# Attention, gated experts and a channel mix on one core: keys split on 128 partitions at once, their halves placed by transfers, and the first batch's steps in a given order

## The chip, the core and the metric

The kernel runs on one core of a Trainium2 chip. The metric is the device time of one execution in microseconds (us). TensorE is called PE, VectorE DVE, ScalarE ACT, GpSimd POOL, and SP is the queue from which nearly all DMA transfers are issued. A change of about 0.5% is what a measurement of this kernel can tell from none.

## What is computed

```python
def sm_attn(qq, kk, vv):
    s = scale * np.matmul(qq, kk.transpose(0, 1, 3, 2))
    a = softmax(s)
    return np.matmul(a, vv)
p_packed = sm_attn(p, k, v)                 # 8 batches, 8 heads, 576 tokens, 32 packed rows
x = sm_attn(q, p_packed, p_packed)          # then heads side by side: 576 x 512 for each batch

for e in range(4):                          # four experts, causal attention of width 64
    q, k, v = x @ wq[e], x @ wk[e], x @ wv[e]
    a = softmax(causal(scale * (q @ k.T)))
    out += gate[e] * (a @ v @ wo[e])        # gate: the two largest of x @ w_gate

xk, xr = mixes of out and out one token earlier (mu_k, mu_r)
k = np.maximum(xk @ w_k, 0.0)
result = sigmoid(xr @ w_r) * ((k * k) @ w_v)
```

All of it is float32. A number is carried as a high part `h` (type fp32r) and a low part `l` = x - h where the kernel writes "split", and a product is then three matmuls: h times h, h times l, l times h.

## The kernel before, in words

The program has two halves. In the first, up to about 400 us, the eight batches pass through these steps, each a Python generator that records its instructions:

- `front(b, g)`, for the two head groups g of a batch: loads, the scores of the packed rows (`eight`, L220), their softmax (L268 to L276, ACT L273), the transposes of the weights (L280) and their copy `aT`, the product with v (L289), `pp` (L296), its transpose (L301) and copy `ppT`; then the second scores `s2` (L220 on `qT`), transposed in blocks by DVE into `st` (L308), block maxima `m` (L311), subtraction (L313), Exp on ACT (L316), `ppT` times the expert weights `wa` (L220 on `wa`, split on ACT L319 and DVE L320 into `PWh` and `PWl`), the block sums (L323 to L328), the scaling (L329), the transposition back into `a2` (L332) and its split into `A2h` (L205) and `A2l` (L335). In batch 0 the subtraction, scaling and split run on DVE and ACT; in the others on POOL.
- `values(b)` (L357): expert values and gate logits, then the gates on DVE.
- `project(b, ep)` (L412), for the two pairs of experts: queries (x = 0), then keys (x = 1), 24 matmuls of 128x288 each into one PSUM tile. The 128 partitions of that tile are two experts of 64. For the keys each expert was copied to `ks` (ACT L430, 64 partitions) and its rest taken to `kl` (DVE L431, 64 partitions), and one transfer for each expert put the high part on the other 64 partitions of `ks` (L433, L434). For the queries, copy and rest go over 128 partitions (L424, L425), and two transfers place the halves.
- `soft(b, e, group)`: causal scores (L472), the masked maximum on DVE (L490), Exp on ACT (L494), and one small transfer, the corner (L501, `ms<-ms`).
- `turn(b, e, group)`: transposes of the weights (L515, and L522 for a block that holds the corner) and their copies `tb`; `pair_out(b, ep)`: the product with the values (L557), its factor (L568, `cx`, `cb`), and differences of tokens to DRAM (L592).
- `fold()`: 24 pieces of w_k and w_r are loaded (`raw`, L775), turned from 64-bit into 32-bit numbers (`decode`, L625 to L655, on DVE, POOL and ACT), split, multiplied by the expert output weights `wo` (L709) and stored.

The second half, from about 400 us on, multiplies with the folded weights (L868, L888, L929) and is not touched but for a buffer.

What sets the order: every step of every generator has a time in a unit of one twentieth of a batch (`FRONT_T`, `G1_T`, `VAL_T`, `PROJ_T`, `SOFT_T`, `TURN_LAG`, `OUT_LAG`, `FOLD_0`, `FOLD_T`) and is recorded in the order of these times, with priorities (`PR`, `PR0`) for the builder's scheduler, which then sets the order of each engine. At run time each engine takes its instructions in that order and waits on semaphores. Before the first loads have landed, PE multiplies zeros (`WARM` times, L168).

## Time and profile before

| | |
|---|---|
| median of 3 runs | 794.79 us (791.86 to 794.84) |
| the profiled execution | 789.45 us |
| its span, first to last instruction | 787.7 us |
| PE busy | 751.6 us (95%) |
| DVE, ACT, POOL busy | 477.4, 448.7, 384.5 us |
| mean granted clock of PE | 0.987 |
| moved by DMA | 148.35 MB |

The profile is of one execution. Its busy times say how long an engine had an instruction in work; a wait names the instruction whose semaphore came last. Two levels of TensorE's clock occur: 1.00 is 2.4 GHz and 0.50 is 1.2 GHz.

### The profile page before, as it was taken

To read this page: it belongs to the slowest core of one execution; us is meant where nothing else is said; L and a number is where in the kernel's file an instruction comes from. 1 tells how busy PE (TensorE), PEld (TensorE's weight loads), DVE (VectorE), ACT (ScalarE), POOL (GpSimd) and SP (SyncE) were. 2 spreads that over 40 slices of the span, in tenths; PEclk is the share of its full clock that TensorE was granted. 3 is DMA by queue.
4 is the path that set the end of the run, shared out by engine and by line. 5 is a ranking of instruction groups with operands and counts; after the bars stand their busy time and mean duration, and the time that the engine had idled before them with its cause. 6 is when DMAs were issued, how large, how long until landed. Compare 5 with 4: busy or idle time off the path is not lost.

```text
span 787.7 us, 15356 instructions
## 1 busy us (share of the span) xinstructions
PE 751.6 (95%) x5504; PEld 617.7 (78%) x5504; DVE 477.4 (61%) x1174; ACT 448.7 (57%) x1029; POOL 384.5 (49%) x484
## 2 busy tenths in 40 slices
PE   6789989999999999998999999999999999999998
PEld 4476968869697887877678888888888888888886
DVE  4979896979868668677767978787581111111111
ACT  2357677678767768786633532422967755555400
POOL 7358776764777635253601533631267443344610
PEclk9599999999999999999999999999999999999999
DMA  9856473655637353315459785867889565555511
GB/s 320 302 151 194 139 226 104 190 151 177 207 105 222 97 166 91 83 43 170 150 201 309 299 296 185 279 196 244 309 286 344 159 187 154 171 177 171 156 67 54
DMA packets 92396, 148.35 MB, mean 188 GB/s; under 512 B 9376, under 2 KB 64160, under 8 KB 90016
## 3 DMA queue, kind: packets, MB, share of 16 engines
q1 hardware_dynamic: 92176, 147.36, 58.7%
q8 instruction: 44, 0.72, 0.4%
q14 instruction: 32, 0.26, 0.1%
q10 hardware_dynamic: 144, 0.00, 0.0%
HBM read 87.04 MB, written 50.33 MB: 174 GB/s over the span
## 4 chain that ended last, share of the span: by engine, by line
PE 74%; DVE 11%; DMA 5%; POOL 4%; ACT 3%; issue 2%; SPq 0%; POOLq 0%; DVEq 0%; ACTq 0%
PE one L929 25%; PE big L888 8%; PE one L888 8%; PE one L557 5%; PE big L412 4%; PE one L868 4%; PE big L868 4%; DMA ms<-ms 4%; PE one L709 3%; PE one L357 3%; PE one L515 2%; PE one L472 2%; DVE ms L490 2%; ACT ms L494 1%; PE big L220 1%
## 5 line engine op out<-in xcount | busy, mean ns | idle before, releaser
L934 DVE TENSOR_TENSOR ring<-one,ring 128x512 f32<-128x512 f32 x36 | 24.9, 692 | 168.3 <-PE one L929 158.8
L929 PE MATMUL one<-wvh,yh 128*128 128x512 f32 x288 | 112.0, 389 | 0.0
L929 PE MATMUL one<-wvl,yh 128*128 128x512 f32 x288 | 112.0, 389 | 0.0
L929 PE MATMUL one<-wvh,yl 128*128 128x512 f32 x288 | 112.0, 389 | 0.0
L494 ACT ACTIVATE ms<-ms,nb 128x192 f32<-128x192 f32 (+3 forms) x128 | 78.4, 616 | 21.3 <-DVE nb L490 21.2
L211 POOL TENSOR_TENSOR yl<-yvh,yh 128x1024 fp32r<-128x1024 f32 (+1 forms) x24 | 49.1, 2060 | 44.7 <-ACT yh L914 24.6
L205 ACT COPY tb<-one 64x128 f32<-64x128 f32 (+5 forms) x208 | 61.4, 362 | 11.3 <-PE one L522 11.2
L640 POOL TENSOR_TENSOR dcx<-dcx,dcu 128x256 f32<-128x256 f32 x40 | 30.7, 768 | 66.1 <-DVE dcu L634 53.5
L929 PEld LDWEIGHTS one<-wvh,yh 128*128 128x128 f32 x288 | 54.1, 188 | 11.3
L929 PEld LDWEIGHTS one<-wvl,yh 128*128 128x128 f32 x288 | 54.1, 188 | 11.3
L929 PEld LDWEIGHTS one<-wvh,yl 128*128 128x128 f32 x288 | 54.1, 188 | 11.1
L211 POOL TENSOR_TENSOR yl<-yvl,yh 128x1024 fp32r<-128x1024 f32 x16 | 38.2, 2396 | 41.0 <-ACT yh L914 19.7
L515 PE MATMUL one<-ident,ms 128*128 128x128 f32 x320 | 53.1, 281 | 3.1 <-ACT ms L494 3.0
L557 PE MATMUL one<-tb,vg 128*64 128x320 f32 (+4 forms) x448 | 53.6, 362 | 0.6 <-DVE nb L490 0.4
L490 DVE CUSTOM_DVE_ANT_0 ms<-one,mstrip 128x192 f32<-128x192 f32 (+2 forms) x96 | 43.5, 481 | 15.9 <-PE one L472 15.2
L557 PEld LDWEIGHTS one<-tb,vg 128*64 128x64 f32 x448 | 33.3, 136 | 18.3 <-issue 1.7
L515 PEld LDWEIGHTS one<-ident,ms 128*128 128x128 f32 x320 | 36.2, 141 | 13.5 <-ACT ms L494 8.3
L211 POOL TENSOR_TENSOR dt<-cb 128x192 f32<-128x192 f32 (+1 forms) x48 | 31.4, 684 | 30.9 <-DVE cb L575 24.2
L1051 ACT ACTIVATE ring<-ring 128x1024 f32<-128x1024 f32 x18 | 19.0, 1059 | 34.9 <-DMA ring<-rscr 34.9
L472 PE MATMUL one<-ks,qs 128*128 128x192 f32 (+3 forms) x128 | 36.6, 300 | 0.4 <-ACT vg L205 0.3
L522 PE MATMUL one<-ident,ms 128*128 128x128 f32 x96 | 27.4, 287 | 9.3 <-DMA ms<-ms 8.7
L661 POOL TENSOR_TENSOR wl<-wc,wh 128x256 fp32r<-128x256 f32 x48 | 34.9, 751 | 0.3
(208 smaller groups left out, 2071.1 us busy)
## 6 DMA issues: line engine op xcount, KB each, us to landing
yscr<-y SPq DMA_DIRECT2D x48, 384.0 KB, 3.5
dl<-dscr SPq DMA_DIRECT2D x40, 256.0 KB, 5.8
yvh<-yscr SPq DMA_DIRECT2D x10, 1024.0 KB, 5.9
kT<-in_k_dram SPq DMA_DIRECT2D x16, 576.0 KB, 4.2
qT<-in_q_dram SPq DMA_DIRECT2D x16, 576.0 KB, 5.7
rscr<-rr SPq DMA_DIRECT2D x12, 768.0 KB, 4.4
ring<-rscr SPq DMA_DIRECT2D x36, 256.0 KB, 2.9
out_dram<-ring SPq DMA_DIRECT2D x36, 256.0 KB, 3.2
```

The lines of the kernel that those rows point to most:

```text
L205: return nc.scalar.copy(o, x)
L211: nc.gpsimd.tensor_tensor(o, x, y, op=op)
L412: nc.tensor.matmul(ps[:, 512 * hf : 512 * hf + SH], ww[:, g, :], xx[:, g, :], start=i == 0, stop=i == 3 * NG - 1,)
L472: nc.tensor.matmul(ps[:, po : po + kn], qs[:, qo : qo + P], keys[:, ko : ko + kn], start=x == 0, stop=x == 1,)
L490: nc.vector.tensor_tensor_reduce(halves(mv) if last else mv, sv, halves(mk) if last else mk, op0=ALU.add, op1=ALU.min, scale=-SC, scalar=3 ...
L494: nc.scalar.activation(to, mv, AF.Exp, bias=nb[:n], scale=-1.0, accum_out=bat["sums"][:n, i, e : e + 1],)
L515: nc.tensor.transpose(ps[:, at + j * P : at + (j + 1) * P], ms[:, j * P : (j + 1) * P], ident)
L557: nc.tensor.matmul(av[64 * ee : 64 * ee + 64, qo - lo : hi - lo], vg[:, j, HD * (2 * ep + ee) : HD * (2 * ep + ee + 1)], tslice(tabs[ee], ...
L661: nc.gpsimd.tensor_sub(l, x, f32(h))
L868: nc.tensor.matmul(po, dx[:, NS * t + s, t0 : t0 + P], wpart("r", s, wx, t), start=n == 0, stop=n == 3 * KT - 1,)
L888: nc.tensor.matmul(po.rearrange("p (b n) -> p b n", b=2), wpart("k0" if f < 4 else "k1", s, wx, t)[:, f % 4 * P : f % 4 * P + P], dx[:, :, ...
L929: nc.tensor.matmul(ps, a[:, f, P * t : P * t + P], wres["v"][b][:, f, :], start=n == 0, stop=n == 3 * NFT - 1,)
```

## The change

The keys: one copy and one subtraction over 128 partitions into `kx` and `lk`, and six transfers for each pair of experts (two for each expert's high part, one for its rest), in place of two copies, two subtractions and two transfers.

```diff
                 if x == 0:
                     z = qt.rearrange("p (e s) -> p e s", e=2)
                     l = ex.tile([P, S], F32R, tag="l", name=nm("l"), bufs=1)
+                    h = z[:, 0, :]
                 else:
-                    z = ks = ex.tile([P, 2, S], F32R, tag="ks", name=nm("ks"))
+                    ks = ex.tile([P, 2, S], F32R, tag="ks", name=nm("ks"))
+                    l, h = (ex.tile([P, S], F32R, tag=n_, name=nm(n_), bufs=1) for n_ in ("lk", "kx"))
+                nc.scalar.copy(halves(h), pv)
+                nc.vector.tensor_sub(halves(l), pv, halves(f32(h)))
                 if x == 0:
-                    nc.scalar.copy(halves(z[:, 0, :]), pv)
-                    nc.vector.tensor_sub(halves(l), pv, halves(f32(z[:, 0, :])))
                     evac(E_Z, z[64:, 1, :], f32(z[64:, 0, :]))
+                    moves = [(z[64:, 0, :], l[:64]), (z[:64, 1, :], l[64:])]
                 else:
+                    moves = []
                     for e in range(2):
                         r = slice(64 * e, 64 * e + 64)
-                        nc.scalar.copy(halves(z[r, e, :]), pv[r])
-                        nc.vector.tensor_sub(halves(kl[r, e, :]), pv[r], halves(f32(z[r, e, :])))
-                top, bot = (l, l) if x == 0 else (z[:, 0, :], z[:, 1, :])
-                nc.sync.dma_start(f32(z[64:, 0, :]), f32(top[:64]))
-                nc.sync.dma_start(f32(z[:64, 1, :]), f32(bot[64:]))
+                        moves += [(ks[:64, e, :], h[r]), (ks[64:, e, :], h[r]), (kl[r, e, :], l[r])]
+                for o, i in moves:
+                    nc.sync.dma_start(f32(o), f32(i))
```

Room for `kx` and `lk` comes from buffers that are now shared: `cb` takes the place of `cx`, `dcu` that of `dce`, and `pp` has one buffer.

The first batch: each of its steps has a time of its own (`OPEN_T0`, `OPEN_T1`), its loads are issued in a list's order, and its instructions on DVE, PE and ACT (`SEQ`) are chained one behind the other in the order in which they are recorded. Head group 0 has its subtraction and scaling on POOL (`SMALL0`). After some steps PE multiplies zeros (`fill`), seven times in all, and there are 10 matmuls of zeros at the start instead of 16. The first four decodings are tied behind named steps of the first batch.

```diff
-PR0, WARM = (1000, 946, 1043, 1073, 1037, 1000, 940, 980, 907), 16
+LOADS = 'k1 k0 q1 q0 v0 v1 wo wa r r'
+TIES_V, TIES_A = [2, 5, -1, 0], [3, 4, 1, 1]
+FILL = [[1, 0, 0, 0, 0, 0], [0, 2, 3, 0, 1, 0]]
+SMALL0 = 'PV'
+SEQ = 'VTA'
+PR0, WARM = (1025, 1000, 970, 1027, 992, 1080, 851, 785, 907), 10
...
+        def seq(b, eng, make):
+
+            with behind(chain.get(eng) if b == 0 and eng in SEQ else None):
+                ins = make()
+            if b == 0:
+                chain[eng] = ins.ins
+            return ins
...
+        def fill(b, g, x, ps, o, ins):
+
+
+            for _ in range(0 if b else FILL[g][x]):
+                with tc.issue_after(ins.ins):
+                    nc.tensor.matmul(
+                        ps[:, o : o + 64], mstrip[:, :P], mstrip[:, P : P + 64], start=True, stop=True
+                    )
```

All the tables of step times are new, too; a line of one of them shows the size of the steps:

```diff
-FRONT_T = [-29.98, -26.81, -23.33, -16.88, -17.51, -14.04, -12.67, -12.1, -8.35]
+FRONT_T = [-33.9, -26.15, -23.1, -17.25, -18.01, -14.57, -12.61, -9.88, -8.72]
```

The line numbers of the changed kernel are higher: L308 is L362 there, L412 L471, L431 L485, L472 L533, L515 L580, L522 L587, L557 L622, L433 L495.

DVE in the first batch, from the factor `pp` of group 1 on. Before:

```order
L296 TENSOR_SCALAR pp_293<-one_272,ri_22_217 128x128
L655 SCALAR_TENSOR_TENSOR wc_326<-dcq_332,dcx_329 128x256
L308 STREAM_TRANSPOSE st_308<-big_299 128x288 x2
L311 TENSOR_REDUCE m_37_311<-st_308 128x18
L313 TENSOR_TENSOR st_308<-st_308,m_37_311 128x576
L625 TENSOR_SCALAR dce_349<-raw_173 128x256
L628 SCALAR_TENSOR_TENSOR dcx_348<-raw_173,dce_349 128x256
L631 TENSOR_SCALAR dce_349<-dcx_348 128x256
L323 TENSOR_REDUCE s_46_342<-st_308 128x9x2
```

The same place in the changed kernel:

```order
L349 TENSOR_SCALAR pp_293<-one_269,ri_22_212 128x128
L362 STREAM_TRANSPOSE st_308<-big_299 128x288 x2
L365 TENSOR_REDUCE m_37_311<-st_308 128x18
L362 STREAM_TRANSPOSE st_325<-big_315 128x288 x2
L365 TENSOR_REDUCE m_40_328<-st_325 128x18
L368 TENSOR_TENSOR st_325<-st_325,m_40_328 128x576
L378 TENSOR_REDUCE s_52_367<-st_308 128x9x2
L688 TENSOR_SCALAR dce_356<-raw_171 128x256
L382 TENSOR_SCALAR r_53_369<-s_52_367 128x18
L691 SCALAR_TENSOR_TENSOR dcx_355<-raw_171,dce_356 128x256
```

Both groups' second scores (`st_308` is group 0, `st_325` group 1) now stand ahead of the first decoding, which had stood ahead of them, and the subtraction of group 0 has left DVE. It stands on POOL, behind the split of `wo` (`won`):

```order
L206 TENSOR_SCALAR woTh<-won_167 128x256 x4
L724 TENSOR_TENSOR woTl<-won_167,woTh 128x256 x4
L368 TENSOR_TENSOR st_308<-st_308,m_37_311 128x576
L386 TENSOR_TENSOR st_308<-st_308,r_53_369 128x576
L703 TENSOR_TENSOR dcx_355<-dcx_355,dce_356 128x256
```

SP in batch 1, the halves of the first pair of experts (`l` and `lk` are rests, `ks` and `kx` high parts of keys, `oo` folded weights). Before:

```order
L723 DMA wscrk_84<-oo_1081 512x1x256
L434 DMA qs_112<-l_1292 64x576
L433 DMA qs_112<-l_1292 64x576
L433 DMA ks_1319<-ks_1319 64x576
L434 DMA ks_1319<-ks_1319 64x576
L775 DMA raw_2371<-in_w_k_dram 128x512
```

Now:

```order
L495 DMA qs_112<-l_1293 64x576 x2
L495 DMA ks_1312<-kx_1314 64x576 x2
L495 DMA kl_114<-lk_1313 64x576
L495 DMA ks_1312<-kx_1314 64x576 x2
L495 DMA kl_114<-lk_1313 64x576
L838 DMA raw_1810<-in_w_k_dram 128x512
```

Two transfers for the keys have become six, the third and sixth of which wait for the subtraction on DVE.

PE in the last batch, from the last key matmul on. Before, the second pair's keys end at the first row here, and 31 matmuls stand between it and their first score:

```order
L412 MATMUL big_5861<-A2h,PWl_4843 128x288 x2
L557 MATMUL one_5889<-tb_125,vg_5029 64x320
L557 MATMUL one_5900<-tb_125,vg_5029 64x256
L557 MATMUL one_5900<-tb_123,vg_5029 64x256
L557 MATMUL one_5889<-tb_123,vg_5029 64x320
```

Now the first pair's scores stand right behind it:

```order
L471 MATMUL big_5890<-A2h,PWl_4785 128x288 x2
L533 MATMUL one_5857<-ks_5750,qs_112 128x192
L533 MATMUL one_5869<-ks_5750,qs_112 128x448
L580 MATMUL one_5881<-ident,ms_117 128x128 x4
L533 MATMUL one_5857<-kl_114,qs_112 128x192
L533 MATMUL one_5857<-ks_5750,qs_112 128x320
```

Between the second pair's last key matmul and its first score stood 31 matmuls before (14 of L557, 5 of L568, 8 transposes, 4 scores); now there are 60.

## Rows read from the trace of the kernel before

**Rows 1.** The page's part 1: engine, busy us (share), instructions.

```profile
PE 751.6 (95%) x5504; PEld 617.7 (78%) x5504; DVE 477.4 (61%) x1174; ACT 448.7 (57%) x1029; POOL 384.5 (49%) x484
```

**Rows 2.** Waits of PE from 34.28 to 400 us: total us, times, longest.

```profile
PE one L522 <- DMA ms<-ms: 8.7, 7, 2.3
PE one L515 <- ACT ms L494: 3.0, 5, 1.5
PE one L301 <- DVE pp L296: 2.0, 2, 1.5
PE big L472 <- DVE l L425: 1.7, 2, 0.9
```

**Rows 3.** Stretches: us; PE, PEld, DVE, ACT, POOL busy; PE clock; DMA; GB/s.

```profile
0.00:34.28 34.28, 21.46 (x263) 13.49 (x264) 23.39 (x61) 11.15 (x22) 18.89 (x44) 0.76 0.94 329
...
365.00:380.00 15.00, 11.35 (x85) 8.46 (x83) 10.35 (x30) 9.23 (x33) 5.45 (x10) 1.00 0.59 175
```

**Rows 4.** The same view around the clock's fall and rise.

```profile
7.58:17.82 10.24, 5.93 (x146) 3.75 (x145) 6.00 (x14) 3.53 (x8) 7.08 (x20) 1.00 1.05 363
17.82:34.28 16.46, 9.57 (x92) 3.77 (x92) 16.00 (x37) 6.13 (x12) 5.37 (x9) 0.50 0.97 347
34.28:38.30 4.02, 4.02 (x18) 4.02 (x19) 3.49 (x10) 1.82 (x4) 2.87 (x4) 0.50 0.62 211
```

**Rows 5.** First batch, order of time: start us, us, instruction, idle before.

```profile
12.45 1.51 POOL L201 TENSOR_SCALAR woTh<-won 128x256 fp32r<-128x256 f32 x4 [2.57 <-DMA won<-in_wo_dram]
13.93 3.06 POOL L661 TENSOR_TENSOR woTl<-won,woTh 128x256 fp32r<-128x256 f32 x4
...
21.06 0.68 ACT L316 ACTIVATE st<-st 128x576 f32<-128x576 f32 x1 [2.05 <-DVE st L313]
...
24.99 0.84 DVE L308 STREAM_TRANSPOSE st<-big 128x288 f32<-128x288 f32 x2
26.41 0.71 DVE L311 TENSOR_REDUCE m<-st 128x18 f32<-128x576 f32 x1
27.16 0.76 DVE L313 TENSOR_TENSOR st<-st,m 128x576 f32<-128x576 f32 x1
32.75 0.77 DVE L332 STREAM_TRANSPOSE a<-st 128x576 f32<-128x576 f32 x1
33.55 0.67 ACT L205 CAST A2h<-a 128x576 fp32r<-128x576 f32 x1 [1.17 <-DVE a L332]
34.28 0.58 PE L357 MATMUL one<-PWh,A2h 128*128 128x260 f32 x1 [0.51 <-ACT A2h L205]
```

**Rows 6.** Loads: SP issue; then that issue's KB and us to landing.

```profile
7.07 0.73 SPq L245 DMA_DIRECT2D vn<-in_v_dram  x1
...
vn<-in_v_dram SPq DMA_DIRECT2D x1, 64.0 KB, 9.4
```

**Rows 7.** POOL groups by line, 34.28 to 400 us: busy us, mean ns.

```profile
L313 POOL TENSOR_TENSOR st<-st,m 128x576 f32<-128x576 f32 x14 | 16.4, 1175 | 18.0 <-DVE m L311 18.0
```

**Rows 8.** DVE groups by line, whole span: busy us, mean ns, idle before.

```profile
L431 DVE TENSOR_TENSOR kl<-big,ks 64x576 fp32r<-64x576 f32 x32 | 24.1, 753 | 14.4 <-ACT ks L430 14.0
...
L425 DVE TENSOR_TENSOR l<-big,qs 128x576 fp32r<-128x576 f32 x16 | 12.0, 752 | 2.1 <-ACT qs L424 1.8
```

**Rows 9.** One key split, batch 5, in order of time, to its first score.

```profile
275.19 0.63 ACT L430 CAST ks<-big 64x576 fp32r<-64x576 f32 x1 [1.16 <-PE big L412]
275.85 0.46 SPq L433 DMA_DIRECT2D ks<-ks  x1
...
277.58 0.76 DVE L431 TENSOR_TENSOR kl<-big,ks 64x576 fp32r<-64x576 f32 x1 [0.97 <-ACT ks L430]
...
281.52 0.33 PE L472 MATMUL one<-ks,qs 128*128 128x192 f32 x1
```

**Rows 10.** The tile ks, all its transfers.

```profile
DMA to landing us min/median/max: 2.2/2.7/6.3
```

**Rows 11.** The chain that ended last, in the last batch: start us, us, what.

```profile
362.84 7.63 DMA ms<-ms
```

More of the change, by code (lines that the diff above doesn't have):

```diff
@@ L207, in evac, with behind, tie, eight @@
                 return nc.vector.tensor_copy(o, x)
-            pool_copy(o, x)
+            return pool_copy(o, x)
         def pool_tt(o, x, y, op):
             nc.gpsimd.tensor_tensor(o, x, y, op=op)
-        def eight(lhs, rhs, n):
+        def behind(ins):
+            return tc.issue_after(ins) if ins is not None else nullcontext()
+        chain = {}
+        def tie(eng, x):
+            return None if x is None or x < 0 else first.get((eng, x)) or chain.get(eng)
+        def seq(b, eng, make):
[4 more added lines that the diff above has]
+            return ins
+        def eight(b, g, x, lhs, rhs, n):
             ps = big()
@@ new lines, in load_v, with load_q, load_first @@
+        def load_v(b, g):
+            vn = vns[(b * NG + g) % 2]
+            nc.sync.dma_start(
+                vn[:, : NT - 1, :], v[b, g, : (NT - 1) * P].rearrange("(c p) x -> p c x", p=P)
+            )
+            nc.sync.dma_start(vn[TAIL:, NT - 1, :], v[b, g, (NT - 1) * P :])
+            return vn
+        def load_q(b, g):
+            qT = ld.tile([P, NH, SH], F32, tag="qT", name=nm("qT"))
+            nc.sync.dma_start(qT, q[b, g])
+            return qT
+        def load_first():
+            got = {}
+            first["raw"] = []
+            for x in LOADS.split():
+                if x == "wa":
+                    for c in range(0, NG * NH, NH):
+                        nc.sync.dma_start(wa[:, c : c + NH, :], w_in[:, c : c + NH, :])
+                elif x == "wo":
@@ L246, in load @@
-                qT = ld.tile([P, NH, SH], F32, tag="qT", name=nm("qT"))
-                nc.sync.dma_start(qT, q[b, g])
-                loaded[b, g] += [vn, qT]
+                elif x == "r":
+                    first["raw"].append(fetch_raw(w_k, len(first["raw"]) * P, 0))
+                else:
+                    got[x] = {"k": load_k, "v": load_v, "q": load_q}[x[0]](0, int(x[1]))
+            for g in range(NG):
+                loaded[0, g] = [*got[f"k{g}"], got[f"v{g}"], got[f"q{g}"]]
@@ L606, in fetch_raw @@
             return raw
-        def behind(ins):
-            return tc.issue_after(ins) if ins is not None else nullcontext()
         def decode(dst, src, r0, f0, raw=None, turn=None):
@@ L621, in decode @@
             t = {
-                m: pools["d"].tile([P, CW], I32, tag="dc" + m, name=nm("dc" + m), bufs=1) for m in "xeuq"
+                m: pools["d"].tile([P, CW], I32, tag="dc" + m, name=nm("dc" + m), bufs=1) for m in "xeq"
             }
-            with behind(first["V", turn] if turn is not None else None):
+            t["u"] = t["e"]
+            with behind(tie("V", turn and TIES_V[turn - 1])):
                 nc.vector.tensor_scalar(
@@ L643, in decode @@
             if E_SQ == "A":
-                with behind(first["A", turn] if turn is not None else None):
+                with behind(tie("A", turn and TIES_A[turn - 1])):
                     nc.scalar.activation(f32(t["q"]), f32(hi), AF.Square)
```

176 lines of the change are left out of this document (93 added, 83 removed).

## The prediction, on record before the changed kernel ran

> **What bounds the kernel now.** I read the page first: PE is busy for 751.6 of 787.7 us, DVE for 61% of the span [rows 1]. The change adds one matmul of zeros to PE's work and takes none of the real ones, so it can only win where PE stands idle or runs at the low clock. The table of stretches shows the places. Until 34.28 us PE is busy for 21.46 us, warm-up and slow matmuls included, and DMA for 0.94 of the time: the first batch goes through its steps with little to fill PE [rows 3]. From there to 400 us the waits of PE name its idle time: the corner transfer, the Exp on ACT, the factor `pp` and the rest of the queries on DVE, 15.4 us in these four rows [rows 2]; some of it lies in the last batch, where PE is idle for 15.00 - 11.35 = 3.65 us of one stretch [rows 3].
>
> The first batch is bound by DVE: between 17.82 and 34.28 us DVE is busy for 16.00 of 16.46 us [rows 4]. Its chain ends with the transposition of group 1's weights at 32.75, the copy into `A2h` at 33.55, and PE's dense work, which begins at 34.28 [rows 5]. The granted clock is 1.00 from 7.58 to 17.82, where PE is busy for 5.93 of 10.24 us, then 0.50 until 38.30; the dense work's first 4.02 us run at 1.2 GHz [rows 4].
>
> **The change, part by part.**
>
> *First batch.* I take the Exp of group 0 as the knot. It ends at 21.06 + 0.68 = 21.74 before, and DVE ends group 1's transposition at 32.75 + 0.77 = 33.52, so 11.8 us of DVE work lie between [rows 5]. In the changed order three pieces of it stand ahead of the Exp: group 1's block transposes, maxima and subtraction, 0.84 + 0.71 + 0.76 = 2.3 us [rows 5]; the scaling of group 0, of the same form as the subtraction and so some 0.76 us, goes to POOL. Of the decoding's instructions seven lay in between before and six do now; I book nothing for that. That leaves 11.8 - 3.1 = 8.7 us.
>
> The Exp itself comes later. Group 0's subtraction waits on POOL for the split of `wo`, which took from 12.45 to 13.93 + 3.06 = 16.99, 4.5 us [rows 5]. `wo` now stands behind 4.0 MB of loads, where the last load of v stood before; that one landed at 7.07 + 9.4 = 16.5 [rows 6]. So POOL is free at 21.0; the subtraction costs 1.2 there [rows 7], and the Exp ends at 21.0 + 1.2 + 0.7 = 22.9, 1.2 us later than before. Group 1's transposition then ends at 22.9 + 8.7 = 31.6, against 33.52: **dense work starts 1.9 us earlier**. Bounds: if POOL or a load is later by one more decoding piece, 0; if group 1 waits for nothing on DVE, 3.1.
>
> The loads of k stay first and the second of them is still the one that group 0 needs, so fewer matmuls of zeros at the start win nothing by themselves. Seven matmuls of zeros cost nothing where they stand, in stretches in which PE waits. The decoding that is pushed back (some one and a half pieces) returns after 34 us; the 128-partition keys of this batch give DVE back what it costs. Nothing booked, and up to 3 us against us at the high end.
>
> *Key split.* Before, one key split is copy, rest, copy, rest: ACT at 275.19, then the second rest on DVE at 277.58, after 0.97 us in which DVE waited; it ends 3.15 us after the first copy began [rows 9]. A subtraction over 64 partitions takes 753 ns and over 128 partitions 752 ns [rows 8], so one of each pair is pure gain: 16 times 0.75 us = 12 us of DVE, and a good part of the 14.0 us that DVE waited for the copies [rows 8]. The PSUM tile comes free at about 0.63 + 0.75 = 1.4 us instead of 3.15. None of this is PE time by itself. What PE gets of it is bounded by the waits that name late DVE or ACT work: 3.0 + 2.0 + 1.7 = 6.7 us [rows 2] above, nothing below. DVE is the engine they lead back to in turn, and it loses a twentieth of its work between 34 and 400 us; I take somewhat less than half, **2.8 us**.
>
> The other side of it: every key now goes through a transfer. In batch 5 the first score came at 281.52, 6.3 us after the first copy [rows 9]. Now: copy 0.63, rest 0.75, its issue some 0.5 behind, landing 2.7 [rows 10], together 4.6 us, so the median transfer leaves 1.7 us of cover, and one like the slowest of before, 6.3 [rows 10], would cost 1.9 us. There are 16 such places, of which the eight of the first pairs have short cover. I book **1.0 us against** the change; bounds 0 and 8 times 1.9 = 15 us.
>
> *Transfers.* 64 more of 144 KB are 9.4 MB on 148. The corner, at 8.7 us the largest wait [rows 2], shares the queue with them. I book **0.5 us against**; bounds: 2 us less, since loads of k are issued earlier now, and 2 us more.
>
> The fastest key transfer landed after 2.2 us and the median after 2.7 [rows 10]. The Trainium skill's page "DMA: Bandwidth & Descriptors" (section "Anatomy of one DMA — SWDGE (gpsimd) path") gives about 2.0 us plus the bytes over 436 GB/s, measured on another issue path, which makes an estimate of 2.3 us for 144 KB. By it the keys would have 2.1 us of cover and the 1.0 us booked against would go; the trace agrees with it for a free queue only.
>
> *Last batch.* In the chain the corner there took 7.63 us from its issue [rows 11], where the median key transfer, nine times its size, took 2.7 [rows 10]. Between the second pair's last key matmul and its first score now stand 60 matmuls instead of 31, so what is late has more to hide behind. Of the 3.65 idle us [rows 3] I take **1.5** off; bounds 0 and 3.
>
> The shared buffers cost nothing that I see: the next writer of each comes far behind the last reader, except `dcu`, where the same instruction reads and writes one buffer in place.
>
> *Sum.* -1.9 - 2.8 + 1.0 + 0.5 - 1.5 = -4.7 us, on the profiled execution's 789.45. That execution is 5.3 us faster than the median of the three runs, 794.79, which is 0.7%, as much as the change itself; I set the sum against the median: 794.8 - 4.7 = **790.1 us**, 0.6% faster. Half a per cent, about what a measurement of this kernel can tell from none, is 4.0 us.
>
> **The rivals.**
>
> *The clock stays up.* Six of the seven matmuls of zeros stand between 9 and 17 us, in the stretch after which the clock fell. If it doesn't fall, or rises sooner, half of 4.02 us is won in the dense work and about 1 us in the first batch's slow matmuls: -4.7 - 3 = 787 us. For it: PE was already busy for 5.93 of 10.24 us there. Against it: the stretch that follows has PE busy for only 9.57 of 16.46 us, at half speed [rows 4], and the change adds next to nothing in it. The page "TensorE: Matmul & The Clock Gate" of the Trainium skill (section "HAM oscillation — how this bites in real kernels") says that gaps between bursts of matmuls bring the low clock back; by that rule the gap that is left after 18 us would undo what the zeros do before it. Rows 4 agree for the kernel before.
>
> *PE's order is the bound, and DVE's lateness was not.* A wait that goes shows the next one: where the key's rest was late, the Exp or the corner is late by nearly as much. Then the 2.8 us and the 1.5 us shrink to some 1 us together, and the time is 794.8 - 1.9 - 1.0 + 1.5 = 793.4 us. For it: the largest wait is a transfer [rows 2] that the key split does not touch.
>
> *Slower: keys that land late.* The place is the first score of the first pair in each batch. If the landing there rises from 2.7 to 5.5 us, because six transfers stand in one queue with the loads, each of eight places waits 5.5 - 2.7 - 1.7 = 1.1 us, and the corner issued behind them as much again: 8 times 2.2 = 17.6, less the first batch's 1.9 and 2.8 for DVE and 1.5 for the last batch: +11, 806 us. It decides at a landing of 4.4 us, 1.7 over the median; at 5.0 the time would be 794.8 - 6.2 + 9.6 = 798 us. For it: the slowest landed after 6.3 us [rows 10]. Against it: in batch 5 the first key transfer was issued at 275.85, 0.03 us after its copy ended, so the queue stood free there [rows 9].
>
> *All late work of DVE goes.* The 6.7 us are won whole and the keys cost nothing: -1.9 - 6.7 - 1.5 = -10, 785 us.
>
> **How the numbers follow.** The forecast has a chance of 0.40, and its size is uncertain by some 3 us, so that 0.28 of it lies beyond 4.0 us and 0.12 within. The clock staying up 0.14, all faster. PE's order 0.24, of which 0.03 faster, 0.20 the same and 0.01 slower. Late keys 0.14, of which 0.02 the same and 0.12 slower. All of DVE's lateness 0.08, faster. Sums: faster 0.53, same 0.34, slower 0.13. The forecast's own range is 786 to 794. The range for 8 times in 10 goes from 781.5 (the clock and DVE's lateness together, 794.8 - 13) to 798.5, which takes in the mild end of late keys and leaves out the rest of them.
>
> **What would show it.** Right: dense work from about 32 us; DVE with 16 subtractions fewer and next to no wait for the key copy; waits of PE on late DVE and ACT work below 5 us; the last batch's idle stretch near 2 us; no wait of the first scores on `ks` or `kl`. The forecast is wrong if dense work starts after 34 us, if the scores wait on the key's transfers by more than 3 us in all, if the corner waits exceed 11 us, or if the second half, which is untouched, differs.

## The result, and the profile after

The changed kernel takes 799.2 us (median of 19 runs, 790.3 to 803.5), the kernel before 793.8 beside it (19 runs, 789.6 to 796.6). The ratio is 1.0069, interval 1.0045 to 1.0092: slower by 5.5 us, where 4.7 us less were forecast. 799.2 lies just above the range of 781.5 to 798.5. The profiled execution took 796.3 us, its span is 794.5: 6.8 us longer than the span of before.

The page's part 1 of the changed kernel, as [rows 1]:

```profile
PE 758.7 (95%) x5506; PEld 624.2 (79%) x5506; DVE 466.9 (59%) x1156; ACT 440.7 (55%) x1013; POOL 382.0 (48%) x486
```

DVE lost 10.5 us of work and ACT 8.0. PE is busy 7.1 us longer with two instructions more (the added matmul of zeros): the real matmuls are the same, and more of them run at the low clock.

The waits of PE from the start of dense work to 400 us, as [rows 2]:

```profile
PE one L587 <- DMA ms<-ms: 9.9, 8, 2.3
PE one L533 <- DVE cb L640: 1.7, 2, 1.6
PE big L471 <- DVE l L485: 1.4, 4, 0.4
PE big L633 <- ACT cx L210: 1.3, 1, 1.3
PE one L580 <- ACT ms L555: 1.3, 3, 0.8
PE big L533 <- DVE lk L485: 1.3, 1, 1.3
```

The late `pp` is gone, and the Exp (`ms` from ACT) is down from 3.0 to 1.3 us. In their place stand the factor `cb`, its copy `cx`, the keys' rest `lk`, and 1.2 us more for the corner.

Stretches (us; PE, PEld, DVE, ACT, POOL busy; PE clock; DMA; GB/s), as [rows 3, 4]:

```profile
0.00:36.24 36.24, 25.51 (x263) 16.51 (x263) 18.24 (x49) 10.78 (x21) 17.73 (x40) 0.88 0.91 309
7.32:24.49 17.17, 14.19 (x186) 9.41 (x186) 5.19 (x15) 3.87 (x9) 6.96 (x19) 1.00 1.05 377
...
27.90:36.24 8.34, 5.28 (x41) 2.38 (x41) 8.32 (x17) 3.18 (x7) 3.87 (x5) 0.50 0.69 219
...
68.86:72.28 3.42, 3.42 (x24) 1.41 (x22) 0.98 (x4) 2.01 (x7) 2.41 (x4) 0.50 0.95 296
365.00:380.00 15.00, 12.05 (x89) 9.44 (x87) 10.13 (x28) 9.14 (x30) 6.92 (x8) 0.98 0.86 239
380.00:400.00 20.00, 18.64 (x109) 16.00 (x108) 15.25 (x38) 12.40 (x41) 9.24 (x14) 0.93 0.44 142
```

Dense work starts at 36.24 us, not at 34.28 as before nor at 32.4 as forecast. The clock column needs care: the profile has no record before 24.49 us and reads 1.00 there, but the matmuls ran slowly. The order of time in the first batch, as [rows 5] (start us, us, instruction, idle before):

```profile
7.32 2.17 PE L241 MATMUL big<-kT,pT 64*32 64x288 f32 x32 [1.07 <-DMA kT<-in_k_dram]
...
17.09 2.77 POOL L724 TENSOR_TENSOR woTl<-won,woTh 128x256 fp32r<-128x256 f32 x4
18.62 1.54 PE L296 MATMUL one<-mstrip 128*128 128x64 f32 x6
20.20 0.35 DVE L349 TENSOR_SCALAR pp<-one,ri 128x128 f32<-128x128 f32 x1 [3.27 <-PE one L296]
20.61 0.47 PE L354 MATMUL one<-ident,pp 128*128 128x128 f32 x1 [0.45 <-DVE pp L349]
21.02 2.17 PE L241 MATMUL big<-qT,ppT 64*32 64x288 f32 x32
24.05 1.16 POOL L368 TENSOR_TENSOR st<-st,m 128x576 f32<-128x576 f32 x1 [4.18 <-DVE m L365]
25.24 0.68 ACT L371 ACTIVATE st<-st 128x576 f32<-128x576 f32 x1 [3.52 <-POOL st L368]
28.88 1.21 PE L241 MATMUL big<-kT,pT 64*32 64x288 f32 x16 [2.99 <-DVE PWl L375]
34.71 0.77 DVE L391 STREAM_TRANSPOSE a<-st 128x576 f32<-128x576 f32 x1
36.24 0.58 PE L416 MATMUL one<-PWh,A2h 128*128 128x260 f32 x1
```

At a granted clock of 0.50 (28.88 us) sixteen score matmuls took 1.21 us; the first 32, at 7.32, took 2.17, and with 16 zeros at the start (below) the same 32 take 1.21. So they ran at the low level, 1.2 GHz. The ten zeros end at 6.25 us and PE stands idle for 1.07 us before the first scores. POOL has ended `woTl` at 19.86 us and then waits 4.18 us for DVE's maxima, which wait for the scores: POOL was not what held the Exp.

The keys of batch 5, as [rows 9]:

```profile
277.12 0.64 ACT L484 CAST kx<-big 128x576 fp32r<-128x576 f32 x1 [0.56 <-PE big L471]
277.94 1.26 SPq L495 DMA_DIRECT2D ks<-kx  x2
278.29 0.74 DVE L485 TENSOR_TENSOR lk<-big,kx 128x576 fp32r<-128x576 f32 x1
281.81 0.60 SPq L495 DMA_DIRECT2D kl<-lk  x1
284.29 0.34 PE L533 MATMUL one<-ks,qs 128*128 128x192 f32 x1
```

One copy, one rest, but now SP takes 4.5 us to issue six transfers, and the first score comes 7.2 us after the copy began (6.3 before). PE finds other work meanwhile.

By landmarks, the changed kernel lags behind by 2.0 us at the start of dense work, by 3.9 at a first score near the end of the seventh batch (342.92 against 339.04 us), by 5.9 at the first matmul with `w_k` in the second half and by 6.8 at the end. The third landmark before and now (the times are those of the first and the last of 48 such matmuls):

```profile
L888 PE MATMUL one<-dh,wk0h x48: 389/389/389, 457.3 to 562.3; 128*128 128x512 f32 x48
L951 PE MATMUL one<-dh,wk0h x48: 389/389/389, 463.2 to 568.1; 128*128 128x512 f32 x48
```

So 2.0 us were lost in the first batch, 1.9 in the batches between, 2.0 from there to the second half, where the last batch lies, and 0.9 in the second half. These are two single executions, and that of the kernel before (789.45 us) was faster than any of its 19 runs: they show where time goes, and the medians how much. From 365 to 400 us PE is idle in the changed kernel for 2.95 + 1.36 = 4.3 us and runs for 3.4 us at the low clock.

### The profile page after: what moved, and what is told of

It is laid out like the page before. It is cut to its first block, busy times and chain, and to the rows that moved or that the text cites. A ratio compares the mean times of both kernels' runs of the same rounds, so it can differ in the third digit from the quotient of the medians.

```text
span 794.5 us, 15424 instructions
## 1 busy us (share of the span) xinstructions
PE 758.7 (95%) x5506; PEld 624.2 (79%) x5506; DVE 466.9 (59%) x1156; ACT 440.7 (55%) x1013; POOL 382.0 (48%) x486
## 4 chain that ended last, share of the span: by engine, by line
PE 68%; DVE 12%; DMA 8%; ACT 5%; POOL 3%; issue 3%; SPq 1%; DVEq 0%; ACTq 0%; POOLq 0%
PE one L992 24%; PE one L951 5%; PE big L951 5%; PE one L622 5%; PE big L471 4%; PE one L931 4%; PE big L931 4%; DMA ms<-ms 3%; PE one L772 3%; PE one L416 3%; PE one L533 2%; PE one L580 2%; DMA raw<-in_w_k_dram 1%; PE big L241 1%; PE big L533 1%
## 5 line engine op out<-in xcount | busy, mean ns | idle before, releaser
L703 POOL TENSOR_TENSOR dcx<-dcx,dce 128x256 f32<-128x256 f32 x40 | 29.9, 748 | 77.2 <-DVE dce L697 62.4
L992 PEld LDWEIGHTS one<-wvh,yl 128*128 128x128 f32 x288 | 54.1, 188 | 11.3
L580 PE MATMUL one<-ident,ms 128*128 128x128 f32 x320 | 54.2, 283 | 1.7 <-ACT ms L555 1.3
L622 PE MATMUL one<-tb,vg 128*64 128x320 f32 (+4 forms) x448 | 50.5, 362 | 0.4 <-DVE nb L551 0.4
L622 PEld LDWEIGHTS one<-tb,vg 128*64 128x64 f32 x448 | 33.8, 137 | 16.3 <-issue 1.2
L580 PEld LDWEIGHTS one<-ident,ms 128*128 128x128 f32 x320 | 36.9, 142 | 10.0 <-ACT ms L555 7.3
L533 PE MATMUL one<-ks,qs 128*128 128x320 f32 (+3 forms) x128 | 37.8, 313 | 1.7 <-DVE cb L640 1.7
L587 PE MATMUL one<-ident,ms 128*128 128x128 f32 x96 | 27.8, 290 | 10.1 <-DMA ms<-ms 9.9
L533 PE MATMUL one<-kl,qs 128*128 128x192 f32 (+3 forms) x128 | 35.5, 318 | 0.0
```

Of the source, the lines that this page charges most:

```text
L533: nc.tensor.matmul(ps[:, po : po + kn], qs[:, qo : qo + P], keys[:, ko : ko + kn], start=x == 0, stop=x == 1,)
L580: nc.tensor.transpose(ps[:, at + j * P : at + (j + 1) * P], ms[:, j * P : (j + 1) * P], ident)
L622: nc.tensor.matmul(av[64 * ee : 64 * ee + 64, qo - lo : hi - lo], vg[:, j, HD * (2 * ep + ee) : HD * (2 * ep + ee + 1)], tslice(tabs[ee], ...
L992: nc.tensor.matmul(ps, a[:, f, P * t : P * t + P], wres["v"][b][:, f, :], start=n == 0, stop=n == 3 * NFT - 1,)
```

## Experiments

Ratios are to runs of the kernel before on the same chip, with 95% intervals. Two theories stood at first: the opening and the last batch lose the time (A), or the key transfers do (B). The later ones are stated where they come in.

### The three parts, each way

The change has three parts: the keys with their shared buffers (K), the first batch (O), and the step times, priorities and choices of engine for all later steps (T). Each of the eight kernels but the two known was run.

| kernel | K | O | T | ratio | interval |
|---|---|---|---|---|---|
| before | - | - | - | 1 | |
| keys alone | K | - | - | 1.0301 | 1.0256 to 1.0346 |
| opening alone | - | O | - | 1.0068 | 1.0039 to 1.0096 |
| times alone | - | - | T | 1.0138 | 1.0100 to 1.0176 |
| times undone | K | O | - | 1.0308 | 1.0267 to 1.0349 |
| opening undone | K | - | T | 1.0136 | 1.0105 to 1.0167 |
| keys undone | - | O | T | 1.0155 | 1.0121 to 1.0190 |
| changed | K | O | T | 1.0069 | 1.0045 to 1.0092 |

Keys alone is the kernel before with the key code of the change, `cb` in the place of `cx`, `dcu` in that of `dce` and one `pp`; keys undone puts the old code back:

```diff
-                nc.scalar.copy(halves(h), pv)
-                nc.vector.tensor_sub(halves(l), pv, halves(f32(h)))
...
+                        nc.scalar.copy(halves(z[r, e, :]), pv[r])
+                        nc.vector.tensor_sub(halves(kl[r, e, :]), pv[r], halves(f32(z[r, e, :])))
```

> The kernel before with the key split over 128 partitions, its transfers and its shared buffers only; opening and step times as before. Theory A (the opening's low clock costs the time in front, the new step times of the last batch the rest; the keys are harmless): 0 to -3 us against the kernel before, ratio 0.996 to 1.000, dense work from 34.3 us as before, DVE some 12 us less busy, first scores wait under 1 us for ks and kl. Theory B (the keys that go through transfers cost the time, by more DMA traffic that makes corners and loads late): +4 to +6 us, ratio above 1.004, with corner waits above 10 us.

> The changed kernel with the key split, its transfers and its shared buffers as before; opening and step times as changed. Theory A: as slow as the changed kernel or slower by up to 3 us, ratio to the kernel before 1.006 to 1.011, DVE some 12 us busier than in the changed kernel. Theory B: as fast as the kernel before, ratio 0.998 to 1.003.

Opening undone gives batch 0 its old times, loads and 16 zeros, and takes away chains and fills; opening alone adds the new ones to the kernel before:

```diff
-FILL = [[1, 0, 0, 0, 0, 0], [0, 2, 3, 0, 1, 0]]
...
+FILL = [[0] * 6, [0] * 6]
...
-SMALL0 = 'PV'
-SEQ = 'VTA'
...
+SMALL0 = 'VV'
+SEQ = ''
```

> The changed kernel with the first batch as before: order of loads, step times of batch 0, no chains, no zeros between steps, 16 zeros at the start, group 0's subtraction on DVE. Theory A: dense work from 34.3 us as before, granted clock 1.00 at 7.6 us, and 2 to 4 us of the 5.5 us lost come back: ratio to the kernel before 1.002 to 1.004; the last batch still 2 to 3 us longer than before. Theory B: no change to the changed kernel beyond the 2 us of the dense work's start, ratio 1.004 to 1.007, and waits spread over all batches.

> The kernel before with the changed first batch only; keys, buffers and all later step times as before. The four runs so far: keys alone ratio 1.030, keys undone 1.016, opening undone 1.014, times undone 1.031. Theory C (each part is set for the others: a part put into the kernel before moves the builder's order of all later work, and waits and low clock come with it): 1.005 to 1.015. Theory D (the opening by itself costs its 2 us of later dense work and no more, as keys alone and times undone, with the opening and without it, were equal): 1.000 to 1.004. Theory A's opening (low clock, 2 to 4 us): 1.003 to 1.005.

Times undone and times alone exchange the tables of all later steps, of which one line:

```diff
-SOFT_T = [1.86, 1.85, 2.56]
+SOFT_T = [1.76, 1.75, 2.48]
```

> The changed kernel with all step times, priorities and evacuation choices outside the first batch as before; keys and opening as changed. Theory A: the last batch's share comes back, 3 us: ratio to the kernel before 1.002 to 1.005, with the dense work still from 36 us; its idle stretch near 370 us as in the kernel before. Theory B: the old times were set for keys that are there 4 us sooner, so the scores wait more: ratio above 1.008.

> The kernel before with the changed step times outside the first batch only; keys, buffers and opening as before. Theory C: slower, 1.010 to 1.030, with more idle time of PE and granted clock 0.50 in several stretches after 40 us. Theory D2 (the new times are simply better, as they take 19 us off a kernel with the new keys): faster, 0.990 to 0.998. Theory A (the new times lengthen the last batch by 3 us): 1.003 to 1.006.

Theory A fell: none of its six ranges held. B's held in two runs (keys alone, above 1.004, though by 24 us and not 4 to 6; times undone, above 1.008) and failed in opening undone and in keys undone, which should have been as fast as the kernel before and is the slower by 1.55%. The keys cost 24 us with the old step times and give back 6.8 (1.0155 to 1.0069) with the new opening and times; the new times cost 11 us without the keys and give back 19 with keys and opening. Every part alone makes the kernel slower. Nothing here adds up. Theory C was made from the first four runs, and the other two, opening alone and times alone, are in its ranges and outside those of A, D and D2.

In the profile of the keys alone PE is busy for 762.7 of 811.2 us, so it is idle for 48.5 us, against 36.1 in the kernel before: of 23.5 us about half is idle time, and half are the same matmuls taking longer. One stretch shows both (order of time, as above):

```profile
150.50 0.83 DVE L688 TENSOR_SCALAR dce<-raw 128x256 int32<-128x256 int32 x1 [0.97 <-DMA raw<-in_w_k_dram]
...
151.49 0.35 POOL L454 COPY gws<-gw 64x4 f32<-64x4 f32 x1 [0.30 <-DVE gw L448]
151.80 1.40 POOL L724 TENSOR_TENSOR wl<-wc,wh 128x256 fp32r<-128x256 f32 x2
151.82 2.10 DVE L452 COPY gws<-gw 64x16 f32<-64x16 f32 x1
153.16 0.72 POOL L784 TENSOR_TENSOR oo<-oo 128x256 f32<-128x256 f32 x1
154.41 0.76 DVE L551 CUSTOM_DVE_ANT_0 ms<-big,mstrip 128x576 f32<-128x576 f32 x1
155.23 0.85 PE L471 MATMUL big<-A2h,PWh 128*128 128x288 f32 x2 [3.71 <-DVE nb L551]
```

and what its clock did behind that:

```profile
154.41:161.24 6.83, 6.01 (x22) 4.36 (x24) 2.98 (x9) 2.15 (x5) 2.35 (x4) 0.50 0.26 70
```

DVE comes early to a decoding whose `raw` has not landed. A copy of 64x16, which mostly takes 0.17 us, then takes 2.10, and ends as POOL's three operations of two inputs end. The masked maximum behind it is late, PE is idle for 3.71 us, and 6.83 us at the low clock follow. The Trainium skill's page "SBUF — State Buffer" (section "Who interferes with whom") says that VectorE and GpSimd share one pair of ports as an exclusive lock, that a copy is among the VectorE operations that can need this pair, and that the one that issues first has it for its whole instruction while the other is blocked. The trace agrees (POOL began at 151.80 us, the copy at 151.82), but the copy lasted through three instructions of POOL, not one.

### Does a copy in POOL's way explain it?

```diff
-            nc.vector.tensor_copy(ws[:64, 1:, :], w[64:, : NT - 1, :])
-            nc.vector.tensor_copy(ws[64:, 1:, :], w[:64, 1:, :])
+            nc.scalar.copy(ws[:64, 1:, :], w[64:, : NT - 1, :])
+            nc.scalar.copy(ws[64:, 1:, :], w[:64, 1:, :])
```

On the keys alone, on the changed kernel, and on the kernel before:

> The kernel with the keys alone (ratio 1.030), and the two small copies of the gates, gws<-gw of 64x16, on ACT instead of DVE. In that kernel one of them took 2.10 us instead of 0.17, from 151.82 to 153.92, while POOL worked without a pause on operations of two inputs from 151.80 to 153.87; the masked maximum behind it came late, PE stood idle for 3.71 us, and the granted clock fell to 0.50 for 6.8 us. Theory G (such collisions of DVE with POOL, and the clock that falls behind the idle time, make the keys alone dear): the idle stretch of 3.7 us near 155 us is gone or under 2 us, and 4 to 8 us of the 24 come back: ratio 1.020 to 1.026. Rival (the next late thing takes its place): 1.027 to 1.033.

> The changed kernel with the two small copies of the gates on ACT instead of DVE; the order is otherwise nearly the same (12 rows on PE). In the changed kernel the copies took 0.17 us but for one of 0.80, so Theory G expects no more than 1 us: ratio 1.004 to 1.008. If the ratio falls below 1.003 or rises above 1.010, small shifts of the order alone are worth as much as the change.

> The kernel before with the two small gate copies on ACT instead of DVE (27 rows of PE's order move). In its profile two of the sixteen copies were long, 0.90 and 0.69 us instead of 0.17, both in the last batch. On the changed kernel the same edit gave 1.0069 to 1.0037, on the keys alone 1.030 to 1.025. Theory G (fewer collisions with POOL): 0.994 to 0.999, faster than both kernels. Theory C (any move of the order costs): 1.002 to 1.010.

Measured: 1.0246 (1.0202 to 1.0290), 1.0037 (1.0007 to 1.0067) and 1.0047 (1.0022 to 1.0071). In the keys alone the ratio is in theory G's range and the idle time shrank as it said, but the next place grew from 1.50 to 3.87 us, as its rival said:

```profile
153.27 0.53 PE L471 MATMUL big<-A2h,PWh 128*128 128x288 f32 x2 [1.01 <-DVE nb L551]
...
172.06 0.37 PE L587 MATMUL one<-ident,ms 128*128 128x128 f32 x1 [3.87 <-DMA ms<-ms]
```

The collision is real, and by the middle values its removal is worth some 4 us there; the intervals with and without it overlap, on the changed kernel too, where the ratio is just below theory G's range. On the kernel before the same edit costs 0.5%: theory G failed there (0.994 to 0.999), and theory C's range held. No version that beats both kernels was found.

### The shared buffers

`cb` takes the tag of `cx`, `pp` one buffer, `dcu` becomes `dce`, in the kernel before:

```diff
-            cb = ex.tile([P, 1 + S], F32, tag="cb", name=nm("cb"), bufs=1)
+            cb = ex.tile([P, 1 + S], F32, tag="cx", name=nm("cb"), bufs=1)
```

> The kernel before with the three shared buffers of the change only (cb in the place of cx, dcu in that of dce, one buffer for pp); keys, opening and times as before. Theory E (what made the keys alone cost 24 us is the shared buffers: cx waits for the last reader of cb, pp for its transposition): most of the 1.030 is here, 1.015 to 1.030, with waits of PE on cx and pp that are 5 us longer than before. Theory C (the order moves): 1.003 to 1.015 with waits spread over other names. My prediction's step (they cost nothing): 0.998 to 1.002.

1.0076 (1.0048 to 1.0104): a quarter of what the keys alone cost, and not the main part. It is in theory C's range; theory E's was missed, and so were its waits: from 36 to 420 us PE waits 3.1 us for `pp` (2.0 in the kernel before) and not once for `cx`.

### Only the order

In the kernel before, two numbers of `PROJ_T` or the three of `SOFT_T` are moved by a tenth, and nothing else; the last run does it on the keys alone.

```diff
-PROJ_T = [-2.04, -1.82, 1.38, 2.56]
+PROJ_T = [-2.04, -1.82, 1.28, 2.46]
```

```diff
-SOFT_T = [1.76, 1.75, 2.48]
+SOFT_T = [1.86, 1.85, 2.58]
```

> The kernel before, with two of its step times (the keys' and the second pair's steps of project) moved by 0.1 of their unit, 0.23 us of a batch of 46 us. No instruction is added, removed or changed; 235 rows of PE's 2,706 stand elsewhere. Theory C (the order is set to this very kernel, and any move of it costs waits and low clock): slower by 3 to 15 us, ratio 1.004 to 1.019. Rival (the order has slack, and what the keys alone cost is a price of the keys): 0.998 to 1.003.

> The kernel before, with the three step times of the scores (soft) moved by 0.1 of their unit, to nearly those of the changed kernel. No instruction is added, removed or changed; 329 rows of PE's 2,706 stand elsewhere, nearly as many as with the keys alone (393). Theory C: slower by 5 to 20 us, ratio 1.006 to 1.025. Rival: 0.998 to 1.003.

> The kernel with the keys alone (ratio 1.030), and the three step times of the scores moved by 0.1 of their unit as in the run on the kernel before (there 1.0081). If the 24 us of the keys alone are chance, one bad order among many: the time falls well below, ratio 1.005 to 1.022. If they are a price that the keys have with the old step times as a whole: 1.025 to 1.037.

1.0074 (1.0046 to 1.0101) and 1.0081 (1.0060 to 1.0101): with the same instructions on the same data, moved times cost as much as the whole change. This decides for theory C against its rival (0.998 to 1.003), as far as it says that a moved order costs time. How it costs is another matter. The waits of PE from 36 to 420 us, all groups added, are 18.8 us in the kernel before and 18.9 with the first nudge. From 41 to 400 us (columns as above; before, then the first nudge) PE is idle for 19.4 and 19.5 us:

```profile
41.00:400.00 359.00, 339.56 (x3495) 280.90 (x3494) 278.32 (x862) 253.10 (x762) 214.40 (x338) 1.00 0.51 150
41.00:400.00 359.00, 339.48 (x3469) 281.25 (x3468) 273.45 (x856) 251.58 (x755) 215.75 (x339) 0.99 0.50 146
```

In these two executions the clock stands for it: the nudged one has three stretches of 3.4 us at 0.50 (from 67.2, 166.2 and 217.4 us), that of the kernel before none after 38.30 us. Over all runs it does not: the six with the nudge have a mean granted clock of 0.980, and so have the 17 of the kernel before beside them. More waits and a lower clock, the way in which theory C has a moved order cost, are therefore not shown for the nudges.

On the keys alone the nudge gave 1.0231 (1.0188 to 1.0274), between the two ranges: by the middle values some 6 of the 24 us went with this one order, and 18 stayed. The intervals overlap, and whether the 18 are a price of the keys or of both orders this one run does not tell. The same copy collided again:

```profile
155.03 1.40 POOL L724 TENSOR_TENSOR wl<-wc,wh 128x256 fp32r<-128x256 f32 x2
155.05 2.09 DVE L452 COPY gws<-gw 64x16 f32<-64x16 f32 x1
156.40 0.71 POOL L784 TENSOR_TENSOR oo<-oo 128x256 f32<-128x256 f32 x1
```

### The opening's zeros

In the changed kernel: 16 zeros at the start; then also without the three in front of group 1's `pp`; then 16 zeros with the gate copies on ACT (edit above).

```diff
-PR0, WARM = (1025, 1000, 970, 1027, 992, 1080, 851, 785, 907), 10
+PR0, WARM = (1025, 1000, 970, 1027, 992, 1080, 851, 785, 907), 16
```

```diff
-FILL = [[1, 0, 0, 0, 0, 0], [0, 2, 3, 0, 1, 0]]
+FILL = [[1, 0, 0, 0, 0, 0], [0, 2, 0, 0, 1, 0]]
```

> The changed kernel with 16 matmuls of zeros at the start instead of 10; on every engine the order of the rest is the same. Theory F (the ten zeros end at 6.25 us, PE then stands idle until 7.32, and the matmuls of the first batch run at 1.2 GHz until 24.5 us, where before they ran at 2.4 from 7.6 to 17.8): the eight score matmuls of a group take 1.2 us again instead of 2.2, dense work starts at 34.5 to 35.5 us instead of 36.24, and 1 to 3 us come back: ratio to the kernel before 1.003 to 1.006. Rival (the clock of the opening costs nothing that lasts, since the first batch waits for DVE and loads): unchanged, 1.006 to 1.009.

> As the run with 16 zeros, and without the three zeros that PE multiplies between group 1's product with v and its transposition (18.62 to 20.17 us in the changed kernel; they write the tile that pp reads, and pp starts at 20.20, 0.03 us after them). Theory F: pp of group 1 and with it the second scores come another 0.8 to 1.5 us earlier, dense work from 33.5 to 34.5 us; ratio 1.000 to 1.005. Rival (the v load, not the zeros, holds the product): second scores at the same time as in the run with 16 zeros, ratio equal to it. A small part of the later order moves with it (33 of some 2,700 rows on PE), which by Theory C may cost or give 2 us.

> The changed kernel with 16 zeros at the start and the two small gate copies on ACT; the order of all engines is nearly that of the changed kernel (8 rows on PE). Dense work at 32.6 us as with 16 zeros, 3.6 us earlier than in the changed kernel. If gains in single places add up: 1.0071 less the 0.003 of the gates alone, 1.003 to 1.005, as fast as the changed kernel with the gates alone or faster. If what is won in front is given back at the corners (with 16 zeros the lead over the kernel before was 2.9 us at 71 us and a lag of 4.6 us at 260): 1.004 to 1.008, with corner waits above 9 us.

Measured 1.0071 (1.0045 to 1.0097), 1.0085 (1.0051 to 1.0118) and 1.0039 (1.0007 to 1.0071). Theory F was right on the scores' time and missed both ratios; the ratio of its rival, that the clock of the opening costs nothing that lasts, held. The third run is in the range for gains that add up and just outside the other, with an interval that takes in both: it decides nothing. The first batch with 16 zeros, in order of time:

```profile
7.49 1.21 PE L241 MATMUL big<-kT,pT 64*32 64x288 f32 x32
...
17.91 1.20 PE L241 MATMUL big<-qT,ppT 64*32 64x288 f32 x32
...
20.44 1.16 POOL L368 TENSOR_TENSOR st<-st,m 128x576 f32<-128x576 f32 x1 [0.28 <-DVE m L365]
...
21.68 0.67 ACT L371 ACTIVATE st<-st 128x576 f32<-128x576 f32 x1
...
32.64 0.58 PE L416 MATMUL one<-PWh,A2h 128*128 128x260 f32 x1
```

Both sets of 32 scores run at 2.4 GHz, the Exp comes 3.6 us earlier, and dense work starts at 32.64 us, 1.64 before that of the kernel before. And the time is the same as with ten zeros. The lead goes in the batches that follow: from 100 to 400 us PE is busy for 281.15 us at a mean clock of 0.97, against 284.33 at 0.99 in the changed kernel (16 zeros, then ten):

```profile
100.00:400.00 300.00, 281.15 (x2869) 231.21 (x2868) 215.77 (x677) 201.24 (x618) 170.17 (x274) 0.97 0.59 167
100.00:400.00 300.00, 284.33 (x2957) 236.86 (x2956) 222.88 (x704) 206.80 (x634) 172.89 (x277) 0.99 0.61 172
```

One of the places, on SP, PE and in the view of DMA from 105 to 117 us:

```profile
110.41 0.47 SPq L564 DMA_DIRECT2D ms<-ms  x1
...
115.85 0.48 PE L587 MATMUL one<-ident,ms 128*128 128x128 f32 x1 [2.79 <-DMA ms<-ms]
```

```profile
q1 hardware_dynamic: 2315, 3.27, 97.0%
...
ms<-ms SPq DMA_DIRECT2D x1, 16.0 KB, 5.4
```

DMA is busy for 0.97 of it, and the corner's 16 KB land after 5.4 us (fastest anywhere: 1.6). Without the three zeros dense work came no earlier (32.59), so these cost nothing once the clock is up; the rival on the second scores was nearer (17.64 against 17.91).

### The corner

On POOL in the changed kernel, and from ACT's queue in the kernel with 16 zeros and the gates on ACT:

```diff
-E_HALF = 'D'
+E_HALF = 'P'
```

```diff
-                        nc.sync.dma_start(*corner)
+                        nc.scalar.dma_start(*corner)
```

> The changed kernel with the corner copied by POOL instead of a transfer (a switch of its own in the change). In the changed kernel PE waits 9.9 us for the corner in 8 places. If the transfer is the bound there, 5 to 9 us come back, ratio to the kernel before 0.996 to 1.001. If the wait moves to the POOL queue or the order moves with it (Theory C): 1.005 to 1.025, with PE waiting for ms from POOL.

> As the run with 16 zeros and the gates on ACT, and the corner's transfer issued from ACT's queue instead of SP's, where it stood behind loads (issued at 110.41 us and landed 5.4 us later in the kernel with 16 zeros, with DMA busy for 0.97 of that stretch). If the queue in front of the corner is what holds it: PE's waits for ms from a transfer below 4 us, and 3 to 6 us come back, ratio 0.996 to 1.002. If the DMA engines themselves are busy, or another late thing takes its place as with the corner on POOL (1.0095): 1.003 to 1.012.

1.0095 (1.0058 to 1.0131) and 1.0164 (1.0133 to 1.0195). On POOL the wait for the corner's transfer is gone from PE's list, and other late work leads it:

```profile
PE big L241 <- DVE r L382: 3.5, 3, 1.3
PE big L241 <- DVE PWl L375: 3.4, 2, 3.0
```

From ACT's queue it grew from 11.3 (16 zeros and gates) to 16.3 us:

```profile
PE one L587 <- DMA ms<-ms: 16.3, 7, 3.8
```

From issue to landing the corner takes 2.6 us in the median from either queue (1.6 to 7.7 from SP's, 1.7 to 7.4 from ACT's). So SP's queue was not what held the corner; but 1.0164 lies above both ranges, and what made this kernel slower than the one with the corner on SP by some 1.2% is not shown. A corner without a transfer wins nothing: 1.0095 is in the range for late work that takes its place, though no wait for `ms` from POOL is in PE's list, as that theory had it. The largest wait of a list is not what its removal is worth.

## Why the prediction was wrong

**The sum.** This is the step that failed first: terms of single places were added as if PE kept what it won there, with no term for the order that the builder makes anew. By the landmarks the first batch came out at +2.0 us (booked: -1.9), the batches between at +1.9 (keys and transfers together: -1.3), the last batch at +2.0 (-1.5) and the second half at +0.9 (nothing). Moving a few step times and nothing else costs 5.9 to 6.4 us; a lead of 3.6 us at the start of dense work left no trace in the time. Where a wait goes, the next one in PE's order grows, and an idle stretch may be followed by one at the low clock, which costs half of its own length on top. That the changed kernel's 5.5 us are the price of its order, and not of its parts, is argued from these runs and not shown: no run has the parts in the old order, since each of them moves it. *PE's order is the bound, and DVE's lateness was not* named the mechanism; its own size, no loss at all, was too mild. It still summed the first batch's gain.

**First batch, -1.9.** Came out as +2.0. "The Exp of group 0 ends at 22.9" failed: it ended at 25.92. The step set POOL's `wo` split as what holds it, and POOL was free at 19.86, a little earlier than the 21.0 assumed: `wo` stands behind 3.7 MB of loads, not 4.0, and landed at 15.5. What held it were matmuls at half speed. "Fewer matmuls of zeros at the start win nothing by themselves" saw that they win nothing, not that they lose the clock (and took group 0's k for the second load of the kernel before, where it is the first). With 16 zeros dense work starts at 32.64, within 0.3 us of the 32.4 forecast. That this is so close is in part luck: there too POOL was free before the maxima came, by 0.28 us, so the split was not the knot; the Exp ended at 22.35 (forecast 22.9), and group 1's transposition 9.53 us later (forecast 8.7). In the changed kernel 9.56 of the 11.8 us from the end of the Exp to that of the transposition remained.

**"Seven matmuls of zeros cost nothing where they stand."** Wrong at the low clock: `pp` of group 1 starts 0.03 us after the last of three zeros that write its tile. With the clock up it was right, as the run without them shows. *The clock stays up* was refuted in the changed kernel's profile: it stayed down.

**Keys, -2.8 and +1.0.** DVE and ACT got their relief (10.5 and 8.0 us), and late `pp`, `l` and Exp fell from 6.7 to 2.7 us, more than was booked. But 4.3 us of waits on `cb`, `cx` and `lk` came instead, and 1.2 at the corner. The keys' own transfers were harmless: PE waited for them for 0.2 us (`ks`); the waits on `lk` name DVE's subtraction. *Late keys*, which held nearly all of the 0.13 that was given to slower, came out on the right side for another reason; its place, the first scores, is not where time was lost. Of the four signs that the forecast is wrong two came, dense work after 34 us and a second half that differs; the other two, waits on the keys' transfers above 3 us and on the corner above 11, did not.

**Transfers, +0.5.** The corner's waits grew by 1.2 us; within the bounds.

**Last batch, -1.5.** Came out as about +2: the lag behind the kernel before grew from 3.9 us (first score near 339 us) to 5.9. Idle time fell from 3.65 to 2.95 us in the one stretch, but behind it 1.36 us came for 0.28, and 3.4 us at 0.50 from 379.5 us cost 1.7. More matmuls in between did hide the corner there; `cb` and `cx` were late instead. That this comes of their one buffer is not shown: keys undone, which has a buffer for each, waits 1.3 us for `cx` as well, though not for `cb`.

**Shared buffers, 0.** Putting them into the kernel before costs 0.8%. PE's waits there do not name them (above), and a nudge that moves rows of PE without any such change costs as much, so it is more likely the order that moves with them; the two were not separated.

**The median.** Setting the sum against the median of the runs and not against the profiled execution was right; that one execution had no low clock after 38.30 us, and every other profile taken here had some.

What stays open: how a moved order costs time, as the nudges show neither more waits nor, over the runs, a lower clock; both nudges went in one direction, and the changed kernel was not nudged. And why the keys with the old step times still cost 18 us after a nudge: all four kernels with these two let DVE wait for the load of one decoding near 150 us, for 1.0 to 2.3 us, and neither the kernel before nor the changed one does. But times alone waits 2.58 us for such a load near 155 us and keys undone 1.34 near 161, so it is a weak sign. The 0.9 us that the untouched second half lost was not looked into. No order was made by hand to see what the parts would be worth in an order of their own.

## What to carry to other kernels

All seven edits made to the kernel before cost time here, from 0.5 to 3.0%, the two that change no work among them. That its step times had been fitted to it is the likely reason, and no run shows it. Where a scheduler sets the order from such times, first measure a nudge: move a number that changes no work. What it costs is the noise of any edit, and a part that is worth less can be judged only with the order fitted again. Count a gain at one place as a gain of the kernel only where the places behind it have slack; and beside each idle stretch of PE, book what the clock may lose after it.

## What the runs showed of the hardware

- The granted clock reads 1.00 until its first record, whatever it was. With ten zeros at the start that record came at 24.5 us and the time of 32 score matmuls nearly doubled unseen (2.17 us for 1.21); in one of six profiles with ten zeros the clock rose at 5.8 us, in the others at 17.8 to 24.8. With 16 zeros it rose between 4.5 and 7.7 us in all.
- Part of the spread of one kernel's runs is the clock. In eleven runs of the kernel before on one chip the time follows the mean granted clock (correlation -0.92), from 790.05 us at 0.985 to 798.19 at 0.975: a mean clock lower by 0.01 is worth 7.9 of 793 us, and the difference is 8.1. In the four other series of this kernel, of 16 to 26 runs, the correlation is only -0.45 to -0.66.
- A low stretch follows an idle one, but not every idle one has a low stretch behind it: 6.83 us at 0.50 came with 3.71 us of idle time in the keys alone, while the kernel before waited up to 2.3 us for a corner and stayed at 1.00 after 38.30 us.
- A DVE copy of 64x16 that mostly takes 0.17 us took 2.10 and 2.09 us where POOL worked on two-input operations without a pause.
